# A new order for the 1551 steps of a clustered attention and gated MLP

## The chip, the cores and the metric

One core of a Trainium2 chip runs the whole kernel as one launch. The metric is device time in microseconds: the median of three runs of the kernel before is 299.8 us (299.25 to 300.07). In the text, PE is TensorE, DVE is VectorE, ACT is ScalarE, POOL is GpSimd and SP is SyncE, which here only issues transfers.

## The reference

There are 4 batches of 8 heads, with 768 tokens of 64 numbers each. Every query and key is assigned to the nearest of 16 centroids of its head, and a query attends only to the keys of its own cluster. The result, as 3072 tokens of 512 numbers, goes through an MLP with a SiLU between two matrices.

```python
q_assign = np.argmax(np.einsum('bhsd,hcd->bhsc', q_n, c_n), axis=-1)
k_assign = np.argmax(np.einsum('bhsd,hcd->bhsc', k_n, c_n), axis=-1)
mask = q_assign[:, :, :, None] == k_assign[:, :, None, :]
scores = scale * np.matmul(q, k.transpose(0, 1, 3, 2))
scores = np.where(mask, scores, -1000000000.0)
scores = scores - np.max(scores, axis=-1, keepdims=True)
attn = np.exp(scores)
attn = attn / (np.sum(attn, axis=-1, keepdims=True) + 1e-09)
attn_out = np.matmul(attn, v)
x = attn_out.transpose(0, 2, 1, 3).reshape(B * S, H * D)
h = x @ w_in                                  # (3072, 512) @ (512, 2048)
out = (h * (1.0 / (1.0 + np.exp(-h)))) @ w_out # (3072, 2048) @ (2048, 512)
```

## The kernel before, in words

The kernel has no loop over its work. It is cut into 1551 small steps, and a text called `plan` (line 722) lists them in the order in which they are issued. The function `step` (line 604) turns each word into instructions. Every engine takes its own instructions in the order of this list, so the plan fixes the order on PE, ACT, DVE, POOL and SP; between engines only semaphores order the work. A word is the step's name and number, then an engine where there is a choice (A for ACT, D for DVE, P for POOL), then one digit for each PSUM bank that the step opens. `qk50` is the score matmul 50, `hi1.A` is done by ACT, `pv4.3` uses bank 3.

A job is the q and k of one head, 128 partitions with 12 rows of 64 numbers each. Jobs k0 to k7 and x0, x1 hold batch 0, h8 to h31 the other 24 heads. A job passes through these steps:

- `r`, `xr` load it in f32, by SP (lines 92 and 94). The eight first jobs are loaded ahead of the plan. The buffers `raw` are few: h jobs share four of them by number modulo 4, and a load waits until `lo` of the job before it in that buffer is done.
- `hi` and `lo` split it into two f16 halves (lines 103 to 107 and 112).
- Jobs of batch 0 are transposed by PE (`tr`, line 135) and copied out of PSUM (`evk`, `evq`). Jobs from h8 on are transposed by the DMA (`ht`, line 121), issued on SP, into the buffer `ab`.
- `L` or `l` computes the 16 logits of every row on PE (line 159), `mx` and `ge` their maximum and a one-hot mark (lines 183 and 192). For h8 to h15, `cm` transposes the marks on PE, `ce` scales them out of PSUM and a transfer on SP puts them below the job in `ab` (line 235). For h16 to h31, `cs` (POOL, line 199), `cx` (a DMA transpose on SP, line 208) and `cv` (a transfer on POOL, line 212) do it. So one matmul yields score and mask.

Attention is cut into units `qk` (PE, line 325), two matmuls each, three units to a head and half of its queries. `ex` (ACT, line 330) takes the exponential; the scores have two PSUM buffers, so `qk` waits until the `ex` two units earlier is done. `vl` loads v (line 264, on SP, or on POOL with P), `v` casts it, `pv` (and its parts `pa`, `pb`, `pc`, `px`, `py`) multiplies (PE, line 342), `nm` divides, and `pt` with `pe`, or for later heads the DMA transpose `xd` on SP (line 381), brings the result into the form that the MLP reads.

The MLP has units `e` (PE, line 390; `a` is the first three quarters of one), `t` (tanh on ACT, line 402) and `g` (DVE, line 405). The second matrix is multiplied in the steps `b` and `bo` for the first two output tiles, and otherwise by a scheme with seven products for pairs of tiles: sums `S`, products `m` (PE, line 477), copies `z` and outputs `o`. `w0` to `w11` load the weights on POOL, each behind a tiny copy that waits for the last `ex` listed ahead of it (line 522). `wc` prepares sums of the second matrix. `j` steps are matmuls on zeros, which fill PE early on.

The transfers of SP go through one DMA queue (q1 in the profile) and those of POOL through another (q0). Both are served by the same 16 DMA engines of the core.

The lines that the steps of the prediction touch: 92 (loads), 121 (DMA transposes of jobs), 159 (logits), 235 (one-hot blocks), 264 (v), 325 (scores), 330 (exp), 526 and 529 (weights).

Of the kernel before, what the change touches and what calls it, by code (L numbers as in the profile page):

```python
# [29 lines left out]
def kernel(  # L30
# [573 lines left out]
    def step(op, n, eng, banks):  # L604
# [138 lines left out]
        t19 e25.2 g19 t25 cm12.1 qk53 ex53 e26.3 g25 v15.D qk54 t26 ex54 ce12.D vl16.P g26 e16.0 t16 e30.2 qk55 ge13
        g16 vl17.P l15.3 ls15 t30 ex55 lo16 r20 qk56 e28.0 t28 ex56 vl14 g30 e17.3 g28 L14.1 qk57 qk58 t17 g17 ex57
        cm13.2 mx14 e31.0 ce13.D ex58 qk59 t31 v9.D mx15 S3 m1.3 ge14 od2 hi17.A ex59 g31 ge15 wc13 pv8.2 cm14 lo17
        r19 ce14.A ht17 qk60 nm8 ex60 S1 qk61 ex61 m7 qk62 ex62 cm15.0 ce15.A wc7 S13 pv9.1 z0 qk63 ex63 S2 nm9 wc14
        v16.D wc9 wc15 wc10 qk64 m11.2 ex64 qk65 m2.0 qk66 ex65 m17 ex66 hi18.P qk67 qk68 lo18 z10 ex67 ht16 vl21.P
        wc11 wc3 S11 v17 S4 m6 pv10.1 ex68 z1 hi20.D qk69 ex69 qk70 ex70 m5 o0 qk71 ex71 l17.0 S12 m16 z2 nm10 z11
        ls17 qk72 vl19.P ht18 vl18.P hi19.A xd8 qk73 l16.0 od1 o3 ex72 r22 r21 ex73 m4 mx17 m15 z12 ls16 mx16 lo19
        qk74 qk75 lo20 v14 xd9 xd10 ge16 o13 pv11.1 nm11 ex74 ex75 ht19 qk76 ex76 m3 pt11.0 m14 S14 o2 r23 qk77 ge17  # L750
        cs16 o1 qk78 ex77 m12.3 qk79 o12 v18.A m13 ex78 qk80 ex79 o11 o10 pv12.3 hi22.D hi21.D lo21 v21 l18.2 ls18
        ex80 qk81 pe11.A ex81 cs17 e35.1 t35 g35 qk82 nm12 e33.0 ex82 qk83 ex83 e32.2 lo22 qk84 ex84 mx18 e34.3 t34
        qk85 g34 t33 g33 pv13.1 ex85 qk86 ex86 ge18 cs18 l19.3 cx16 nm13 e36.0 ht20 vl20 ls19 t32 g32 vl22 t36 g36
        qk87 ex87 cx17 ht22 hi23.D e37.1 qk88 t37 g37 mx19 xd12 ex88 cx18 e40.3 ht21 t40 lo23 cv16 g40 cv17 e39.0 qk89
        ex89 t39 e41.2 ht23 l20.1 qk90 ex90 ls20 mx20 g39 qk91 ge20 t41 ex91 g41 pv14.3 vl24.P e38.1 t38 g38 qk92 ex92
        qk93 nm14 e43.2 t43 ge19 g43 ex93 e42.0 l22.1 ls22 xd13 cs19 qk94 ex94 xd14 cx19 e44.3 mx22 t42 g42 cs20 qk95
        ex95 e46.1 l21.2 ls21 t46 g46 qk96 qk97 S23 pv15.0 ex96 cx20 qk98 r25 e47.1 mx21 ge21 e45.2 t44 cv18 nm15 g44
        ex97 qk99 ex98 t47 xd15 v22 t45 qk100 cs21 g47 g45 m21.0 ex99 ex100 v19.D ge22 l23.1 qk101 ls23 m22.2 z20
        qk102 ex101 ex102 qk103 ex103 m27.1 qk104 pv16.3 ex104 cv19 qk105 qk106 ex105 S21 S22 mx23 o20 v20 ex106 m26
        z21 S24 ge23 e48.2 t48 cx21 qk107 ex107 r24 cs22 cx22 cv20 qk108 nm16 m25 z22 o23 vl23.P pv17.3 cs23 hi24.D  # L760
        xd16 qk109 cx23 v23.D cv21 ex108 qk110 m23 cv22 ex109 g48 nm17 o21 m24 o22 ex110 qk111 lo24 ht24 e49.2 ex111
        qk112 e50.1 cv23 t49 vl25.P ex112 g49 qk113 xd17 e51.3 v24 t50 ex113 qk114 g50 e52.2 t51 pv18.0 ex114 g51 t52
# [67 lines left out]
```

## Time and profile before

| what | value |
|---|---|
| time, median of three runs | 299.8 us |
| span of the profiled execution | 297.9 us |
| instructions | 8577 |
| PE, matmuls | 3433, mean clock 1.000 |
| DMA bytes | 44.13 MB, 75208 packets |
| DMA queue q1 (SP) | 35.75 MB, 50.3% of 16 engines over the span |
| DMA queue q0 (POOL) | 7.54 MB, 13.5% |

The time of a run is a little more than the span, which goes from the first to the last instruction of one profiled execution; only that execution has a trace. A row of a group or a timeline gives the start in us, the duration in us (for several instructions in a row, from the first start to the last end), the engine, the line of the kernel, the operation, what is written and read, and the count. Matmuls overlap: the duration of one is longer than the distance to the next. A bracket at the end of a row says how long the engine was idle and what released it. In the chain of work that ended last, rows have the start, the length and the step. In the stretches, each engine's busy time stands with its number of instructions, and the DMA share is the mean busy share of the 16 DMA engines. In rows of DMA queues stand the packets, the MB and the share of 16 engines in that stretch. In rows of issues stand the number of transfers, the size of one and the median time from issue to landing.

### The profile page before, as it was taken

To read this page: it belongs to the slowest core of one execution; us is meant where nothing else is said; L and a number is where in the kernel's file an instruction comes from. 1 tells how busy PE (TensorE), PEld (TensorE's weight loads), DVE (VectorE), ACT (ScalarE), POOL (GpSimd) and SP (SyncE) were. 2 spreads that over 40 slices of the span, in tenths; PEclk is the share of its full clock that TensorE was granted. 3 is DMA by queue.
4 is the path that set the end of the run, shared out by engine and by line. 5 is a ranking of instruction groups with operands and counts; after the bars stand their busy time and mean duration, and the time that the engine had idled before them with its cause. 6 is when DMAs were issued, how large, how long until landed. Compare 5 with 4: busy or idle time off the path is not lost.

```text
span 297.9 us, 8577 instructions
## 1 busy us (share of the span) xinstructions
PE 288.7 (97%) x3433; PEld 212.6 (71%) x3433; DVE 223.8 (75%) x489; ACT 233.2 (78%) x406; POOL 68.7 (23%) x124
## 2 busy tenths in 40 slices
PE   7899999999979999999999999999999999999995
PEld 3767766666658887777866887767867886777684
DVE  5898849689979986989467897788656733666663
ACT  5998999965979878999789876898669768964731
POOL 2655804000227001334444024220420000000000
PEclk9999999999999999999999999999999999999999
DMA  6999999999997899795399535867221102211103
GB/s 214 286 256 247 179 201 176 193 247 216 171 300 178 171 176 257 176 151 131 102 202 213 164 66 114 256 165 113 51 89 35 26 2 74 82 29 35 39 19 125
DMA packets 75208, 44.13 MB, mean 148 GB/s; under 512 B 54288, under 2 KB 70960, under 8 KB 75168
## 3 DMA queue, kind: packets, MB, share of 16 engines
q1 hardware_dynamic: 70272, 35.75, 50.3%
q0 software_dynamic: 4608, 7.54, 13.5%
q8 instruction: 27, 0.44, 0.6%
q10 hardware_dynamic: 288, 0.30, 0.3%
q14 instruction: 13, 0.11, 0.1%
HBM read 27.30 MB, written 6.29 MB: 113 GB/s over the span
## 4 chain that ended last, share of the span: by engine, by line
PE 87%; DMA 5%; ACT 3%; DVE 3%; issue 1%; SPq 0%; ACTq 0%
PE ph L390 25%; PE pS L325 20%; PE xb L477 18%; PE pO L342 12%; PE psN L159 4%; PE yb L477 3%; PE po L417 2%; DMA ab<-cd 2%; DMA ab<-hl 1%; DMA raw<-in_q_dram 1%; DVE hl L112 1%; PE wb L477 1%; ACT P L330 1%; ACT hl L103 1%; PE pTq L135 1%
## 5 line engine op out<-in xcount | busy, mean ns | idle before, releaser
L330 ACT ACTIVATE P<-pS 128x768 f16<-128x768 f32 x192 | 151.0, 815 | 18.8 <-PE pS L325 17.4
L390 PE MATMUL ph<-xt,win_s 128*128 128x384 f16 x512 | 96.1, 326 | 0.0
L405 DVE SCALAR_TENSOR_TENSOR gt<-tn,ph 128x384 f16<-128x384 f32 x128 | 68.2, 549 | 31.9 <-ACT tn L402 31.0
L325 PE MATMUL pS<-ab 128*128 128x384 f16 x384 | 86.7, 326 | 2.2 <-DMA ab<-cd 1.6
L402 ACT ACTIVATE tn<-ph 128x384 f32<-128x384 f32 x128 | 61.6, 499 | 13.9 <-PE ph L390 10.5
L390 PEld LDWEIGHTS <-win_s 128*128 128x128 f16 x512 | 49.4, 98 | 31.0 <-issue 0.3
L325 PEld LDWEIGHTS <-ab 128*128 128x128 f16 x384 | 34.2, 98 | 18.3 <-DMA ab<-cd 2.2
L342 PEld LDWEIGHTS <-P 128*128 128x128 f16 x1152 | 39.8, 97 | 3.8 <-DVE cd L234 0.4
L342 PE MATMUL pO<-vt,P 128*128 128x65 f16 x1152 | 41.2, 193 | 0.0
L477 PEld LDWEIGHTS <-gt 128*128 128x128 f16 x352 | 34.1, 98 | 6.5
L112 DVE SCALAR_TENSOR_TENSOR hl<-raw,hl 128x768 f16<-128x768 f32 (+3 forms) x35 | 32.0, 916 | 0.8 <-ACT hl L103 0.5
L105 POOL TENSOR_SCALAR hl<-raw 128x768 f16<-128x768 f32 (+1 forms) x9 | 19.5, 2167 | 47.2 <-DVE gt L405 30.7
L477 PEld LDWEIGHTS <-s 128*128 128x128 f16 x264 | 25.5, 98 | 4.7
L199 POOL TENSOR_SCALAR od<-od 128x96 f16<-128x96 f16 x16 | 8.4, 526 | 63.3 <-DVE od L192 63.2
L499 ACT ACTIVATE ot<-xb 128x256 f32<-128x256 f32 x33 | 12.7, 385 | 12.9 <-PE xb L477 12.6
L477 PE MATMUL xb<-wout_s,gt 128*128 128x256 f16 x176 | 22.6, 273 | 0.0
L159 PEld LDWEIGHTS <-ab 128*128 128x128 f16 x544 | 18.9, 97 | 4.1 <-DMA ab<-hl 0.5
L477 PE MATMUL xb<-wc,s 128*128 128x256 f16 x160 | 20.7, 272 | 0.0
L159 PE MATMUL psN<-stk,ab 128*128 128x16 f16 (+1 forms) x544 | 20.1, 184 | 0.1
L354 DVE TENSOR_TENSOR xn<-pO,zr 128x384 f16<-128x384 f32 x32 | 17.8, 557 | 1.1
L490 DVE TENSOR_TENSOR s<-gt 128x1024 f16<-128x1024 f16 x22 | 15.5, 712 | 1.3 <-PE xb L477 1.0
L212 POOL DMA_DIRECT2D ab<-cdt x16 | 9.0, 564 | 19.8 <-PE pS L325 5.2
(93 smaller groups left out, 258.2 us busy)
## 6 DMA issues: line engine op xcount, KB each, us to landing
raw<-in_k_dram SPq DMA_DIRECT2D x31, 192.0 KB, 3.9
raw<-in_q_dram SPq DMA_DIRECT2D x24, 192.0 KB, 3.5
out_dram<-ot SPq DMA_DIRECT2D x18, 256.0 KB, 2.9
vn<-in_v_dram SPq DMA_DIRECT2D x19, 192.0 KB, 4.7
vn<-in_v_dram POOLq DMA_DIRECT2D x13, 192.0 KB, 3.4
win_s<-in_moe_w_in_dram POOLq DMA_DIRECT2D x8, 256.0 KB, 6.8
wout_s<-in_moe_w_out_dram POOLq DMA_DIRECT2D x4, 512.0 KB, 9.2
out_dram<-ot SPq DMA_DIRECT2D x12, 128.0 KB, 1.8
```

What stands on the lines that cost most here:

```text
L105: nc.gpsimd.tensor_scalar(out=o, in0=i, scalar1=QS, scalar2=None, op0=ALU.mult)
L112: nc.vector.scalar_tensor_tensor(out=hl[:, s, 1, :], in0=raws[job.name][:, s, :], scalar=QS, in1=hl[:, s, 0, :], op0=ALU.mult, op1=ALU.sub ...
L159: nc.tensor.matmul(L[:, n % 2, :, n // 2], ab[:, i, :], stk[:, job.groups[i // 3][0], x : x + w], start=(x == 0), stop=(x + w == 2 * HC),)
L325: nc.tensor.matmul(pS[:, e, 0:HALF], abs_[kj.name][:, kn, :], rhs, start=True, stop=True)
L330: nc.scalar.activation(out=P, in_=pst.pop(u)[:, :, 0:HALF], func=AF.Exp, bias=0.0, scale=ESC)
L342: nc.tensor.matmul(o[:, (2 * t + h) * VW : (2 * t + h + 1) * VW], Ps[i + h, c, j // 2][:, j % 2, ts(t, 128)], vtb[(i + h) % 13][:, j, 0:VW ...
L354: nc.vector.tensor_tensor(out=xn, in0=ov[:, :, 0:D], in1=zr.unsqueeze(2).to_broadcast([128, 2 * NM, D]), op=ALU.mult)
L390: nc.tensor.matmul(ph[:, 0:HALF], win_s[:, r, ts(fb, 128)], xts[b, c][:, r, :], start=(r == 0), stop=(r == NR - 1))
L402: nc.scalar.activation(out=tn, in_=phs[b, c, fb][:, 0:HALF], func=AF.Tanh, bias=0.0, scale=0.5)
L405: nc.vector.scalar_tensor_tensor(out=gt[:, fb, NM * c : NM * c + NM, :].rearrange("p t n -> p (t n)"), in0=tns.pop((b, c, fb)), scalar=1.0 ...
L477: nc.tensor.matmul(o, self.lhs(l, f), self.rhs(r, f), start=(f == 0 and opens), stop=(f == HB - 1), skip_group_check=True)
L490: nc.vector.tensor_tensor(out=o, in0=a, in1=b_, op=op)
```

## The change

The plan is replaced by another list of the same 1551 steps. Each step keeps its engine; the order and the PSUM banks differ. Two rules that depended on the order are made free of it: the three buffers of one-hot marks go to jobs in a fixed turn, and the five buffers of v go to the next load in the order in which they come free.

```diff
+    turn = """
+        k0 k1 k2 k3 k4 k5 k6 k7 x0 x1 h8 h10 h9 h11 h12 h13 h14 h15
+        h16 h17 h18 h20 h19 h21 h22 h23 h24 h26 h25 h27 h28 h29 h30 h31
+    """.split()
...
     def ge_n(job):
         m = (job.n + 1) // 2
-        nn[job.name] = len(nn)
+        nn[job.name] = turn.index(job.name)
...
-    vts, vns = {}, {}
+    vts, vns, vn_slot = {}, {}, {}
+    vn_free = list(range(5))
 
     def load_v(i, eng=nc.sync):
-        vn = mp.tile([128, NJ, D], f32, name="vn", bufs=5)
+        vn_slot[i] = vn_free.pop(0)
+        vn = mp.tile([128, NJ, D], f32, name="vn", tag=f"vn{vn_slot[i]}", bufs=1)
...
         vts[i] = vt
+        vn_free.append(vn_slot[i])
```

The first lines of the old plan, up to the third `ht`, and of the new one, up to the fourth:

```diff
-        j2.1 hi1.A lo1 vl3 hi2.D vl5 vl0 tr0.32 j2.0 evq0.A r8 vl1 evk0.A c5.12 stk lo2 vl4 kad tr1.03 L0.2 hi4.P w0
-        j2.1 mx0 ge0 evq1.A hi3.A lo3 evk1.A ct0.32 ctk0 tr2.10 ctq0 hi5.A evk2.A L1.3 lo4 xr0 evq2.A tr3.21 evq3.A
-        qk0 ex0 mx1 L2.0 ge1 ct1.13 ctq1 evk3.D qk1 ex1 L3.2 mx2 ge2 cm2 ce2.A ctk1 lo5 xr1 tr4.13 evk4.D evq4.A mx3
-        qk2 qk3 hi7.P v0 ge3 L4.0 mx4 ge4 tr5.31 ex2 qk4 v3.A ex3 hi6.P lo6 r10 vl7 cm3 evq5.D evk5.D ce3.A cm4 ce4.A
-        qk5 tr6.23 evk6.D ex4 L5.1 v5 evq6.D j1.2 qk6 vl2 L6.2 vl6 mx5 r9 r11 w1 lo7 tr7.03 ex5 ge5 qk7 xh0.A ex6 mx6
-        evk7.A ex7 qk8 cm5 ex8 xl0 ge6 cm6 ce5.D xq0.0 ce6.D evq7.D xp0.1 xu0.D qk9 xw0.D v1 vl12 ex9 v4 v7 pa0.3 qk10
-        w3 L7.1 w7 qk11 ex10 ex11 xL0.0 xM0 mx7 ge7 cm7 pb0 qk12 xm0 xg0 xh1.D ce7.A v2 xc0 pc0 xe0.D ex12 qk13 pa1.0
-        qk14 pc1 nm0 pt0.3 w2 ex13 qk15 xl1 w5 v6.D pb1 hi8.D nm1 ex14 qk16 ex15 qk17 ex16 ex17 hi10.P w10 xq1.1 xp1.2
-        xu1.D qk18 qk19 pa2.0 pb2 w6 w4 od0 v12.D xw1.D ex18 qk20 pt1.2 hi9.D pe1.D pc2 nm2 ex19 qk21 xL1.2 ex20 w8
-        xM1 ex21 qk22 qk23 pt2.0 ex22 ex23 xm1 px3.1 qk24 pe0.D lo8 xg1 xc1 py3 qk25 ex24 qk26 pe2.D a1.0 xe1.A nm3
-        pt3.1 pe3.D a0.2 ex25 ex26 qk27 ex27 e1 e4.1 e0 t4 g4 vl10 qk28 t0 g0 qk29 ex28 e6.3 t6 g6 ex29 vl11.P e3.1 t3
-        w9 t1 e5.2 qk30 ex30 w11 g3 lo9 r13 vl8 qk31 t5 pv4.3 qk32 ex31 nm4 e8.1 g1 g5 qk33 ht8 lo10 hi11.P e14.0 ex32
-        ex33 t14 g14 qk34 t8 ex34 qk35 e11.2 e13.3 ht10 g8 wc4 wc5 t11 g11 r12 ex35 t13 g13 qk36 ex36 e10.1 e15.0 qk37
-        pt4.2 qk38 e2.3 t10 ex37 ex38 lo11 pe4.D ht9 r14 pv5.2 g10 t15 nm5 qk39 qk40 t2 ex39 ex40 e7.1 e12.2 t12 ht11
...
+        vl1 hi1.A lo1 j2.0 j2.2 vl0 tr0.03 evq0.A evk0.A c5.12 kad stk tr1.30 hi3.A hi2.D lo2 hi4.P L0.1 mx0 ge0
+        evq1.A evk1.A tr2.20 evk2.A vl3 evq2.A ct0.13 ctq0 lo3 ctk0 lo4 L1.2 vl4 tr3.30 hi5.A xr0 qk1 r9 mx1 evq3.A
+        evk3.D ex1 L2.1 qk2 w0 vl2 ge1 hi6.P mx2 lo5 hi7.P L3.0 ct1.23 ex2 ge2 cm2 ctq1 qk0 mx3 ge3 cm3 j1.2 ctk1
+        ce2.A ce3.A w1 tr5.12 ex0 tr4.30 v3.A lo6 qk5 qk4 evq5.D evk5.D vl7 v1 evk4.D evq4.A xr1 tr6.21 ex5 L4.0 ex4
+        lo7 evk6.D v0 mx4 ge4 qk3 ex3 L5.3 mx5 cm4 ce4.A evq6.D L6.2 v4 ge5 cm5 ce5.D vl6 qk7 vl5 tr7.01 qk8 r8 pa0.3
+        w3 mx6 xh0.A ex7 evk7.A ge6 pc0 w7 w2 cm6 ex8 xl0 qk10 ex10 evq7.D L7.0 ce6.D qk11 mx7 xp0.1 ge7 ex11 v2 xu0.D
+        qk6 cm7 xq0.2 xh1.D ce7.A w5 pb0 qk9 xL0.1 w10 w6 xw0.D nm0 xM0 xm0 ex6 w4 ex9 qk15 ex15 w8 r10 pa1.0 qk16 pb1
+        w9 xg0 xc0 qk14 v5 ex16 xl1 ex14 pc1 xe0.D vl11.P hi9.D nm1 qk17 ex17 j2.1 r11 qk12 ex12 hi8.D v6.D xp1.2 qk13
+        ex13 xq1.3 pt0.1 xu1.D xw1.D qk20 ex20 xL1.2 qk18 ex18 pt1.3 lo9 pe1.D xM1 qk22 ex22 pa2.0 qk19 pb2 ex19 qk21
+        ex21 pc2 vl8 pe0.D qk23 ex23 px3.1 xm1 r13 xg1 nm2 lo8 qk24 ex24 pt2.0 pe2.D v7 py3 qk27 hi10.P ex27 nm3 ht9
+        hi11.P a0.3 xc1 xe1.A qk26 vl15 ex26 pt3.1 qk25 ex25 lo10 pe3.D e4.2 t4 g4 e0 t0 g0 e6.0 w11 t6 g6 v8.D qk28
+        ex28 ht8 a1.1 e1 lo11 qk29 e8.3 ht10 ex29 t8 vl13 qk32 ex32 e11.2 qk34 ex34 g8 t11 g11 e5.0 t5 hi13.D t1 g1
+        qk31 ex31 pv4.3 nm4 ht11 e15.2 t15 g5 qk38 ex38 qk42 ex42 g15 r12 e14.1 l9.3 t14 ls9 vl10 qk35 lo13 ex35 e13.0
+        t13 e3.3 t3 qk30 L8.2 ex30 g14 g13 qk33 ex33 e9.1 g3 e7.3 t9 mx8 ge8 cm8 mx9 t7 g9 g7 qk37 vl9 ex37 ge9 ce8.A
+        r14 qk36 e2.0 t2 g2 pv5.1 nm5 ex36 L11.2 hi12.A mx11 qk40 e10.3 v13.A qk43 ex40 b0.0 ge11 cm11 ex43 wc8 r15
...
```

Further down, the places that the prediction names, in the old list and in the new one:

```diff
-        hi12.A lo12 vl13 ht12 wc12 b4.3 ce10.A ex46 pt6.2 b5 cm9.0 ex47 hi14.A ce9.A pe6.A lo14 r16 pv7.1 nm7 b6 ht14
-        pt5.0 pe5.D qk48 hi15.D lo15 ht15 v10.D pt7.1 pe7.A r17 ex48 b7 bo1 e24.0 e18.1 t24 g24 t18 L11.2 wc8 mx11 g18
-        ge11 e22.3 t22 hi16.P e21.0 t21 g22 v11.D v8.D g21 qk49 qk50 cm11 ce11.D ex49 ex50 l12.3 vl9 ls12 e29.1 r18
...
+        lo12 wc9 t10 r17 v15.D ht12 vl18.P vl12 pt4.1 v10.D pe4.D qk39 ex39 b1 g10 qk44 pt5.1 ex44 qk46 ex46 L10.3
+        wc12 pe5.D ht13 qk41 ex41 e12.1 t12 mx10 ce11.D qk47 ex47 pv6.2 b2 hi14.A wc13 hi15.D ge10 cm10 qk45 ce10.A
...
+        ge12 l13.3 bo0 wc5 v11.D ht15 pt7.1 pe7.A ls13 b6 lo14 hi17.A qk57 ex57 b7 cm9.3 ce9.A lo17 ht17 cm12.1 bo1
...
```

More of the change, by code (lines that the diff above doesn't have):

```diff
@@ L743 @@
[L743 to L762, printed above, removed]
@@ new lines @@
+        ex92 g40 qk95 ex95 nm14 ge19 cs19 l21.1 ls21 cv18 e47.2 qk94 cx20 mx21 t47 vl22 e44.3 t44 ex94 g47 e45.0
+        hi24.D t45 g44 ge21 xd12 cx19 xd14 cs21 g45 e37.1 t37 xd13 cv19 vl20 qk96 e38.3 g37 ex96 cx21 t38 hi25.P g38
+        e42.2 t42 lo24 qk97 qk101 ex97 e43.0 r26 pv15.3 t43 ex101 v19.D qk99 ex99 S23 nm15 e46.1 t46 g42 qk100 mx22
+        ex100 g43 m21.3 qk104 ex104 l23.0 g46 qk98 ls23 m22.2 ht24 S21 S22 qk106 xd15 S24 cv21 ex98 qk102 ge22 ex106
+        z20 pv16.0 cv20 o20 ex102 lo25 qk107 ex107 cs22 cx22 mx23 m26 z21 qk111 ex111 nm16 ge23 r29 v22 e51.1 t51
@@ new lines @@
+        qk112 m25 m27.2 g51 z22 o23 cs23 ex112 cx23 qk105 ex105 m23 qk120 v20 ex120 cv22 o21 e53.0 hi27.D lo27 qk103
+        ex103 t53 g53 m24 o22 qk109 vl23.P hi26.P e49.1 ex109 t49 e52.3 g49 t52 g52 pv17.0 ht25 qk110 r28 ex110 nm17
+        l24.3 cv23 ls24 mx24 lo26 xd16 qk116 ex116 e55.2 t55 qk115 ex115 g55 e50.3 t50 g50 r30 xd17 qk117 ex117 e48.1
+        t48 g48 e62.2 qk113 ex113 qk108 e54.0 e56.1 e63.3 v23.D ex108 t54 t56 qk129 t63 g54 ex129 g56 ht27 vl25.P
+        qk131 ex131 ge24 g63 pv18.0 hi29.D e58.1 r31 t58 nm18 m41.3 ht26 qk118 qk119 g58 t62 ex118 vl29.P g62 ex119
@@ L795 @@
+        e118.3 t118 g115 t112 g112 g118 m83 e114.1 o81 t114 e127.0 t127 g114 g127 e113.2 t113 e120.3 g113 t120 g120
+        e119.1 e124.0 e121.2 e126.3 t119 g119 t124 g124 S93 t121 g121 e122.1 t126 g126 e125.0 t122 e123.2 t123 g122
+        t125 m91.3 m97 g123 g125 S91 S92 m101.2 m102.1 z90 m96 S103 m107.0 z100 S101 o100 z91 m95 z92 S94 S102 m106
+        m93 z101 m105 S104 z102 o91 o93 o103 m92.1 o90 m103 o101 m104 o102 m94 o92
     """.split()
```

75 lines of the change are left out of this document (40 added, 35 removed).

## The prediction

> **What bounds the kernel now.** I read the page first, then the chain that ended last, then the engines' shares in stretches of 10 us, then the DMA queues by stretch, and last the timelines of PE and SP around each place where PE waited.
>
> ```profile
> span 297.9 us, 8577 instructions
> PE 288.7 (97%) x3433; PEld 212.6 (71%) x3433; DVE 223.8 (75%) x489; ACT 233.2 (78%) x406; POOL 68.7 (23%) x124
> ```
>
> The sum is made against this span; the three runs have a median of 299.8 us, so 1.9 us lie around it, which I keep. PE is the bound and works in order, so what can change is how late it runs against its own work. The next rows, from the chain and from PE's timeline, price that work: the distance from one start to the next.
>
> ```profile
> 69.09 0.18 PE px L363 x3
> 90.24 1.10 PE pO L342 x36
> 277.00 5.20 PE ph L390 x32
> 293.55 0.89 PE xb L477 x8
> ```
>
> ```profile
> 58.16 1.03 PE L417 MATMUL po<-wout_s,gt 128*128 128x512 f16 x4
> 59.02 0.49 PE L325 MATMUL pS<-ab 128*128 128x384 f16 x2
> 59.35 0.76 PE L159 MATMUL psN<-stk,ab 128*128 128x16 f16 x24
> 59.95 1.02 PE L417 MATMUL po<-wout_s,gt 128*128 128x512 f16 x4
> ```
>
> A matmul of ph or pS costs 0.163 us, of pO 0.030, of po 0.215, of xb, yb or wb 0.109, a logit 0.025, a transpose 0.056; the whole plan comes to 280.1 us. I call a step's place the PE work listed ahead of it, and its lag the time at which it ran less its place. L8, the first logits of the second batch, has 149 transposes and the like, 208 logits, 90 pS, 216 pO, 64 ph, 8 po and 7 filling matmuls ahead: place 48.3. It ran at 59.35, a lag of 11.1. The last matmul ends at 294.4, a lag of 14.3, and 3.5 us of output follow: 280.1 + 14.3 + 3.5 = 297.9. Only the lag is to be won or lost. Where it grew:
>
> ```profile
> 64.16 0.51 PE L159 MATMUL psN<-stk,ab 128*128 128x32 f16 x12
> 74.83 0.52 PE L159 MATMUL psN<-stk,ab 128*128 128x32 f16 x12
> 87.46 0.82 PE L325 MATMUL pS<-ab 128*128 128x384 f16 x4 [1.57 <-DMA ab<-cd]
> ```
>
> l9 (place 53.0) ran with a lag of 11.1, l12 (63.3) with 11.6, qk57 (74.1) with 13.3. So the lag is made before 59 us and at one wait at 85.7; from 87.46 to the end it grows by 1.0. What feeds PE in that time is the DMA:
>
> ```profile
> core 0: us, PE busy (x) PEld busy (x) DVE busy (x) ACT busy (x) POOL busy (x), PEclk, DMA share, GB/s
> 0.00:10.00 10.00, 7.70 (x63) 3.87 (x63) 6.61 (x31) 6.15 (x12) 3.49 (x13) 1.00 0.74 229
> 10.00:20.00 10.00, 9.33 (x177) 7.37 (x176) 8.89 (x24) 9.73 (x18) 6.28 (x10) 1.00 0.96 289
> 20.00:30.00 10.00, 9.21 (x178) 7.07 (x177) 9.16 (x22) 8.62 (x12) 5.57 (x13) 1.00 1.00 233
> 30.00:40.00 10.00, 9.76 (x162) 7.20 (x161) 7.82 (x18) 9.38 (x13) 6.32 (x11) 1.00 1.02 174
> 40.00:50.00 10.00, 9.96 (x91) 6.33 (x90) 7.29 (x14) 9.72 (x19) 4.09 (x5) 1.00 1.00 197
> 50.00:60.00 10.00, 10.00 (x113) 6.51 (x111) 7.46 (x17) 9.42 (x17) 0.00 (x0) 1.00 1.18 192
> ```
>
> Its share is about 1.0 from 10 to 60 us: the 16 engines have no time to spare. PE hardly shows it, because the old list asks PE for each thing about when the DMA can have brought it.
>
> **The change part by part.** Both lists hold the same 1551 steps, each on the same engine with the same buffers' sizes. No work is added or removed; order, PSUM banks and slots differ.
>
> *Scores more evenly spaced.* Until the first MLP matmuls, exp on ACT paces PE. ACT's waits from 22 to 37.5 us in the old kernel:
>
> ```profile
> ACT P L330 <- PE pS L325: 1.1, 4, 0.6
> ```
>
> There the PE work from one qk to the next jumps between 0.3 and 1.4 us (qk16, qk17, qk18 at places 20.4, 20.7, 21.7); in the new list it is 0.6 to 1.1 from qk11 on. I credit 1.0 us; bounds 0 and 1.1.
>
> *The wait at 85.7 us.* It is an SP queue. DVE had written this one-hot block (h11) by 75.9; SP issued its transfer only at 82.05, behind two DMA transposes, a load and an output:
>
> ```profile
> 75.41 0.47 DVE L234 TENSOR_SCALAR cd<-psN,kadd 96x256 f16<-96x256 f32 x1
> ```
>
> ```profile
> 75.25 5.13 SPq L121 DMA_TRANSPOSE ab<-hl  x2
> 82.05 0.60 SPq L235 DMA_DIRECT2D ab<-cd  x1
> ```
>
> The new list has ht12 and ht13 ahead of ce11 on SP, but both stand well before it, and 8.9 us of PE work between ce11 and its first score (10.9 before). I credit 1.6 us, with bounds of 0 and 1.7.
>
> *Jobs of the second batch pulled forward: the cost.* ht9, ht8, ht10 and ht11 stood at places 41.6, 35.9, 38.5 and 44.6; they now stand at 27.4, 30.6, 32.2 and 35.5, and PE meets l9 at 37.5 (53.0 before), L8 at 39.8 (48.3), L11 at 44.5 (60.6). Place 44.5 is 148 transposes and the like (8.2), 244 logits (6.2), 80 pS (13.0), 216 pO (6.5), 56 ph (9.1) and 7 filling matmuls (1.5). Will the DMA have served them by then? Prices from the DMA queues by stretch: 0 to 30 us (loads on q1), 30 to 50 us (weights on q0), 56 to 59 us (transposes alone).
>
> ```profile
> q1 hardware_dynamic: 6017, 6.26, 65.8%
> ```
>
> ```profile
> q0 software_dynamic: 2297, 2.95, 87.9%
> ```
>
> ```profile
> DMA packets 2620, 0.69 MB, mean 231 GB/s; under 512 B 2600, under 2 KB 2619, under 8 KB 2619
> ...
> q1 hardware_dynamic: 2613, 0.67, 128.2%
> ```
>
> A load costs 0.658 x 30 / 6.26 = 3.15 us of all 16 engines per MB, a weight 0.879 x 20 / 2.95 = 5.96 us per MB, a transpose of 1536 packets 1.282 x 3 / 2600 x 1536 = 2.3 us. Sizes:
>
> ```profile
> raw<-in_k_dram SPq DMA_DIRECT2D x31, 192.0 KB, 3.9
> vn<-in_v_dram SPq DMA_DIRECT2D x19, 192.0 KB, 4.7
> win_s<-in_moe_w_in_dram POOLq DMA_DIRECT2D x8, 256.0 KB, 6.8
> wout_s<-in_moe_w_out_dram POOLq DMA_DIRECT2D x4, 512.0 KB, 9.2
> ```
>
> A head's q and k (two rows of 192 KB) cost 1.24, a v 0.62, all twelve weights 25.0. Old list, up to and with ht9, the third transpose: the first 8 jobs 7.4, x0 and x1 2.5, six r 7.4, twelve v 7.4, eight small one-hot blocks 1.2, weights 25.0, three transposes 6.9: 57.8 us. It landed here:
>
> ```profile
> L121 SPq DMA_TRANSPOSE ab<-hl x1: 2146/2146/2146, 58.8 to 58.8; - x1
> ...
> DMA to landing us min/median/max: 4.6/4.6/4.6
> ```
>
> So 57.8 us of listed work were done at 63.4: 5.6 us for the start, for holes and for the landing. New list, up to and with ht11: 7.4 + 2.5 + five r 6.2 + twelve v 7.4 + 1.2 + 25.0 + four transposes 9.2 = 58.9. With the same 5.6 that is 64.5, and L11 then has a lag of 20.0. Two things can make it earlier: w10, w8 and w9 stand at places 17.0 to 18.7 (21.0, 24.5 and 32.2 before), which can fill holes of the DMA, and w11 (3.1 us), listed at 30.3 behind hi10 and hi11 on POOL, can end behind ht11. The other weights will not make room. With both queues at work, q0 gets the larger part (48 to 54 us):
>
> ```profile
> q0 software_dynamic: 696, 0.70, 79.6%
> q1 hardware_dynamic: 461, 0.58, 31.9%
> ```
>
> The bounds are a lag of 15.5 (holes filled and w11 behind) and 20.0. I take 17.5, nearer to the middle, since the one row of this kind (63.4) has neither help. The wait comes in three or four pieces, at l9, L8 and L11, and at DVE's v8, lo11 and hi13, which stand in order behind the loads vl8, r11 and r13; gates queue behind those. The two gains above lie ahead of these waits or depend on the same DMA, and are swallowed. After L11 the list asks the DMA for less than it can serve.
>
> *Slots.* v's slot now comes from the earliest cast. Any waiting there is small already, and I put it at 0:
>
> ```profile
> SPq L264 <- DMA vn<-in_v_dram: 1.3, 1, 1.3
> ```
>
> The one-hot slots by a fixed turn and the other banks I put at 0 too; the cover is the 3 us or more of PE work between a slot's last reader and its next writer (cm8 at 42.0, ge11 at 47.3 in the new list). Without it, each would cost a fraction of a microsecond.
>
> *Sum.* Lag 17.5 after L11 in place of 13.3 after qk57, then the same 1.0: 280.1 + 18.5 + 3.5 = 302.1, and with 1.9 around it 304.0 us.
>
> **The rivals.** *The DMA keeps up (faster).* If the transposes land before PE asks, the gains stand: 297.9 - 1.0 - 1.6 = 295.3, or 297.2 us. It decides at l9: ht9 would have to land by about 47.6 (place 37.5 and a lag of 10.1). For it: nothing requires weights to be first. Against it: 79.6% to 31.9%, and the ledger.
>
> *It cancels (same).* From 47 to 60 us the transposes of the old kernel took:
>
> ```profile
> DMA to landing us min/median/max: 4.6/10.0/11.1
> ```
>
> If ht11 takes no more than 11.1, issued by SP at its place with the old lag (35.5 + 11.1 = 46.6), L11 runs at 57.7, a lag of 13.2, and 280.1 + 14.2 + 3.5 + 1.9 = 299.7.
>
> *PE cools down (slower still).* PE starts at half rate:
>
> ```profile
> 1.18 3.59 PE L538 MATMUL junk<-zz 128*128 128x512 f16 x8 [1.18 <-DVE zz L547]
> ```
>
> That is 0.45 us for a matmul of 512 columns against 0.215 for po. Should a long wait bring this back, it costs about half of 3.6 us once, 1.8: 305.8 us. The wait of 1.57 us above did not: the matmuls behind it have full rate. The Trainium skill, "TensorE: Matmul & The Clock Gate", Part 1, says that an idle window of about 3.4 us halves the clock until PE has been busy as long; by that rule a single wait over 3.4 us would do it, which no row of this trace can show.
>
> *Nothing of this is reached*, because order on POOL holds weights back: that falls under the first two.
>
> **How the numbers follow.** Forecast without cooling 0.48, with it 0.17, cancelling 0.10, DMA keeps up 0.25. A measurement of this kernel tells about 0.3%, 0.9 us. Faster 0.25, same 0.10, slower 0.65. The range goes from 297.2, the middle of the fast case, to 307.0, the upper bound of the lag (280.1 + 21.0 + 3.5 + 1.9 = 306.5) with some cooling. The slower case alone runs from 302 to 307.
>
> **What would show it.** Right: PE waits at psN for ab<-hl (L159) between 45 and 66 us, of 5 to 8 us in all; L11's 24 logits start at about 62; DVE waits for raw or vn near 40 to 48 us; a transpose takes over 11 us to land. Wrong: no wait of PE for ab<-hl, and L11 at 55; then the DMA served q1 ahead of the weights. The even spacing is right if ACT waits under 0.3 us for pS from 22 to 37 us.

## The result and the profile after

The new order takes 314.86 us (median of four runs, 314.01 to 322.95), the old one 299.52 us (299.09 to 300.07). The ratio is 1.0509, with a 95% interval of 1.0477 to 1.0541: slower by 15 us. (The run of 322.95 us is over 1.5% above the fastest of its kernel, so the median counts it and the ratio does not; the profiled execution of e3 below, of 316.45 us, is of the same kind.) The profiled execution of after took 315.52 us, with a span of 313.4 us. The head of its page:

```profile
span 313.4 us, 8562 instructions
PE 292.8 (93%) x3433; PEld 214.6 (68%) x3433; DVE 225.4 (72%) x489; ACT 234.7 (75%) x406; POOL 70.1 (22%) x124
```

PE has the same 3433 matmuls and 15.5 us more in which to run them. The stretches of 10 us say where (columns: stretch, its length, busy time of each engine, granted clock of PE, share of the DMA engines, GB/s):

```profile
core 0: us, PE busy (x) PEld busy (x) DVE busy (x) ACT busy (x) POOL busy (x), PEclk, DMA share, GB/s
30.00:40.00 10.00, 7.59 (x111) 5.81 (x110) 4.89 (x12) 6.30 (x10) 5.26 (x8) 0.83 1.13 243
40.00:50.00 10.00, 9.76 (x115) 6.64 (x112) 7.43 (x14) 9.55 (x17) 3.12 (x3) 1.00 1.25 204
50.00:60.00 10.00, 4.23 (x33) 2.36 (x30) 2.61 (x6) 3.36 (x6) 0.00 (x0) 0.78 1.24 197
60.00:70.00 10.00, 10.00 (x127) 6.62 (x125) 7.75 (x18) 8.16 (x15) 0.30 (x1) 0.88 0.56 143
```

Two stretches lose most of it, 30 to 40 and 50 to 60 us, and in both the clock is below 1.00. PE's timeline there, with the logits of heads 9, 8 and 11 behind (a bracket is the idle time before the row, and what ended it):

```profile
31.50 0.33 PE L371 MATMUL px<-ident,xn 128*128 128x128 f16 x3
34.24 0.50 PE L333 MATMUL pS<-ab 128*128 128x384 f16 x2 [2.41 <-DMA ab<-cd]
...
35.90 0.80 PE L333 MATMUL pS<-ab 128*128 128x384 f16 x2
36.49 0.87 PE L350 MATMUL pO<-vt,P 128*128 128x65 f16 x12
...
38.47 0.55 PE L333 MATMUL pS<-ab 128*128 128x384 f16 x2
...
50.08 0.81 PE L398 MATMUL ph<-xt,win_s 128*128 128x384 f16 x4
56.66 1.46 PE L333 MATMUL pS<-ab 128*128 128x384 f16 x4 [5.77 <-DMA ab<-cd]
57.92 1.49 PE L398 MATMUL ph<-xt,win_s 128*128 128x384 f16 x4
59.20 0.85 PE L159 MATMUL psN<-stk,ab 128*128 128x32 f16 x12
...
62.77 0.49 PE L333 MATMUL pS<-ab 128*128 128x384 f16 x2
63.10 0.75 PE L159 MATMUL psN<-stk,ab 128*128 128x16 f16 x24
...
67.83 0.76 PE L159 MATMUL psN<-stk,ab 128*128 128x16 f16 x24
```

Both waits are for one-hot rows of batch 0 (`ab<-cd`): at 34.24 for head 6, at 56.66 for the job x1. Behind each the matmuls run at half rate for a while (the granted clock is 0.50 from 36 to 38 and from 56 to 62 us): from 56.66 to 62.77 there are 18 matmuls of pS and ph and 12 logits, 3.2 us by the prices of the prediction, in 6.1 us, so 2.9 us are lost; from 35.90 to 38.47 it is 1.2 us. What x1's row waited for stands in SP's timeline, and in the landings of the first transpose and of the row:

```profile
36.52 8.07 SPq L121 DMA_TRANSPOSE ab<-hl  x1
44.70 0.70 SPq L240 DMA_DIRECT2D ab<-cd  x1
...
46.13 11.57 SPq L121 DMA_TRANSPOSE ab<-hl  x2
...
58.43 1.42 SPq L121 DMA_TRANSPOSE ab<-hl  x1
```

```profile
L121 SPq DMA_TRANSPOSE ab<-hl x1: 8075/8075/8075, 36.5 to 36.5; - x1
...
DMA to landing us min/median/max: 19.9/19.9/19.9
L240 SPq DMA_DIRECT2D ab<-cd x1: 702/702/702, 44.7 to 44.7; - x1
...
DMA to landing us min/median/max: 11.9/11.9/11.9
```

The transpose of head 9 (ht9) is listed just ahead of x1's row. It holds SP for 8.07 us and lands at 36.5 + 19.9 = 56.4; the row behind it is issued at 44.70 and lands at 56.6. In the old list no transpose of the second batch stood ahead of that row. Three smaller waits follow. The first and the last are for transfers; the second, of 0.54 us, is for DVE:

```profile
133.41 0.52 PE L159 MATMUL psN<-stk,ab 128*128 128x32 f16 x12 [1.50 <-DMA ab<-hl]
156.53 0.50 PE L333 MATMUL pS<-ab 128*128 128x384 f16 x2 [0.99 <-DMA ab<-cdt]
```

The account of PE's time: waits 2.4 + 5.8, half rate 1.2 + 2.9, later waits 1.5 + 0.5 + 1.0, and 0.8 more between the last matmul and the end, less the 1.6 us wait at 85.7 that is gone: 14.5 of the 15.5 us. The rest is in pieces under 1.3 us.

### The profile page after: what moved, and what is told of

The parts are those of the page before. It is cut to its first block, busy times and chain, and to the rows that moved or that the text cites. A ratio compares the mean times of both kernels' runs of the same rounds, so it can differ in the third digit from the quotient of the medians.

```text
span 313.4 us, 8562 instructions
## 1 busy us (share of the span) xinstructions
PE 292.8 (93%) x3433; PEld 214.6 (68%) x3433; DVE 225.4 (72%) x489; ACT 234.7 (75%) x406; POOL 70.1 (22%) x124
## 4 chain that ended last, share of the span: by engine, by line
PE 75%; DMA 13%; SPq 5%; DVE 3%; issue 2%; ACT 1%; POOL 1%; POOLq 0%; DVEq 0%; ACTq 0%
PE ph L398 22%; PE xb L485 17%; PE pS L333 16%; PE pO L350 10%; DMA ab<-cd 7%; PE psN L159 3%; PE yb L485 3%; PE po L425 2%; DMA ab<-hl 2%; DMA ab<-cdt 1%; DMA raw<-in_k_dram 1%; SPq L389 1%; SPq L213 1%; SPq L271 1%; PE wb L485 1%
## 5 line engine op out<-in xcount | busy, mean ns | idle before, releaser
L398 PE MATMUL ph<-xt,win_s 128*128 128x384 f16 x512 | 99.6, 330 | 0.3 <-DVE xt L382 0.2
L333 PE MATMUL pS<-ab 128*128 128x384 f16 x384 | 90.6, 331 | 9.2 <-DMA ab<-cd 8.2
L350 PEld LDWEIGHTS <-P 128*128 128x128 f16 x1152 | 40.5, 98 | 4.3 <-issue 0.7
L350 PE MATMUL pO<-vt,P 128*128 128x65 f16 x1152 | 42.0, 194 | 0.0
L507 ACT ACTIVATE ot<-xb 128x256 f32<-128x256 f32 x33 | 12.6, 385 | 15.7 <-PE xb L485 15.5
L107 DVE TENSOR_SCALAR hl<-raw 128x768 f16<-128x768 f32 (+1 forms) x16 | 10.8, 684 | 9.1 <-DMA ab<-hl 6.6
```

Of the source, the lines that this page charges most:

```text
L333: nc.tensor.matmul(pS[:, e, 0:HALF], abs_[kj.name][:, kn, :], rhs, start=True, stop=True)
L350: nc.tensor.matmul(o[:, (2 * t + h) * VW : (2 * t + h + 1) * VW], Ps[i + h, c, j // 2][:, j % 2, ts(t, 128)], vtb[(i + h) % 13][:, j, 0:VW ...
L398: nc.tensor.matmul(ph[:, 0:HALF], win_s[:, r, ts(fb, 128)], xts[b, c][:, r, :], start=(r == 0), stop=(r == NR - 1))
L507: nc.scalar.activation(out=o, in_=self.xb[:, 0:DH], func=AF.Copy, bias=0.0, scale=0.5)
```

## The experiments

Each run has a short name, e1 to e18. In the diffs a line holds steps of the list; a time without "before" beside it is a median, and each ratio is to the kernel before, run on the same chip at the same time. The theory: more transfers are listed ahead of the first readers than the DMA queues carry, so PE waits at whichever reader comes first. The main rival: two or three unlucky places in the order, on SP or on VectorE.

**The code without the order (e1).** The old list in the new code, so that only v's queue and the slots differ.

> The list of steps of before in the code of after: only the buffers of v from a queue and the fixed turn of the one-hot slots are new. Theory (all of the time is in the order of the list): 299.5 us, within 0.3% of before. Rival (the queue hands out a buffer of v that is still waited for, and a load behind it on SP or GpSimd is late): over 300.5 us, with more idle time of GpSimd at the lines that load v.

299.76 us, 1.0005 [0.9977, 1.0032]. All of the change's time is in the list.

**Is it the place of one transpose?** First ht9 behind x1's row (e3):

```diff
- nm3 ht9 hi11.P a0.3 xc1 xe1.A qk26
+ nm3 hi11.P a0.3 xc1 xe1.A ht9 qk26
```

> After with one step moved: the DMA transpose of head 9 goes behind the one-hot row of x1 on the SP queue, in place of ahead of it. Rival (one transfer stands in front of another on one queue, which is all that ails the order there): x1's row is issued at 42.5 us in place of 44.70 and without the transpose ahead of it, the 5.93 us wait at 50.57 us and the slow matmuls behind it (2.9 us) go, 306 to 309 us. Theory (what is listed by then is more than the queues carry): the wait moves to the logits of head 9 and 8, which need the transposes, and at least half of it stays: 310 to 315 us.

311.04 us, 1.0391 [1.0354, 1.0428], in the theory's range: by the ratios 3.5 of the 15 us came back. Its trace is left aside. In after something else waits at that place too, on DVE (waits from 36 to 62 us):

```profile
DVE hl L107 <- DMA ab<-hl: 6.6, 1, 6.6
```

The buffer that `hi13` writes is free when ht9 has landed, and gates of batch 0's MLP queue on DVE behind it. So e16 moves this step as well:

```diff
- e5.0 t5 hi13.D t1 g1 ... vl10 qk35 lo13
+ e5.0 t5 t1 g1 ... vl10 qk35 hi13.D lo13
```

> After with the transpose of head 9 behind x1's row on SP, and the high half of head 13 moved on VectorE from ahead of the gates of blocks 1 and 5 to its low half's place, 3 us of TensorE work later: so nothing of batch 0 stands behind the second batch's transposes any more at 49 us. Theory (more is listed than the queues carry, whichever step waits for it first): the wait moves on to the logits of head 9 or 8, at 51 to 56 us, 4 us or more, 308 to 312 us. Rival (the two places where batch 0 stands behind these transposes are the loss): no wait over 2 us between 45 and 65 us, 302 to 306 us.

316.07 us, 1.0553 [1.0492, 1.0615]: no gain over after. The wait has moved on, to the logits of head 9:

```profile
59.26 0.82 PE L159 MATMUL psN<-stk,ab 128*128 128x32 f16 x12 [6.36 <-DMA ab<-hl]
```

Freed of both places, PE runs into the transposes themselves. It is at l9 at the same time as in after (59.26 and 59.20 us). The time is above the theory's range, the place and the size of the wait are as it said; the rival with its 302 to 306 us is out. Why e16 takes 5 us more than e3, which has only the first of its two moves, stays open.

**Is it the amount?** The order of after, with fewer bytes of weights (e5):

```diff
-  wout_s[:, 4 * r : 4 * r + 4, :],
-  moe_w_out[512 * r : 512 * r + 512, :].rearrange("(c p) d -> p c d", p=128),
+  wout_s[:, 4 * r, :], moe_w_out[512 * r : 512 * r + 128, :]
+  nc.gpsimd.memset(wout_s[:, 4 * r + 1 : 4 * r + 4, :], 0.0)
```

> After with the four loads of w_out cut to a quarter (one block of rows in four; the other blocks are set to zero on GpSimd, and the last product is computed with these zeros, so three quarters of w_out are left out of the result). No step moves. The three loads that fall before 50 us shrink by 7.8 of the 10.4 us that they have in the ledger of transfers. Theory (too many bytes are listed ahead of the one-hot rows of batch 0): x1's row and the transposes of head 9 and 8 land several us earlier, the 5.93 us wait at 50.57 us falls below 2 us, with its slow matmuls gone: 303 to 308 us. Rival (the order on the SP queue by itself: a transpose issues for 8 us whatever else moves): the wait stays over 4 us, 312 to 316 us.

308.92 us, 1.0336 [1.0289, 1.0383]. The 5.8 us wait for x1's row is gone, with nothing moved. SP's timeline of this kernel:

```profile
38.00 2.98 SPq L121 DMA_TRANSPOSE ab<-hl  x1
44.10 0.58 SPq L240 DMA_DIRECT2D ab<-cd  x1
45.42 4.06 SPq L121 DMA_TRANSPOSE ab<-hl  x2
```

ht9 holds SP for 2.98 us in place of 8.07, the next two for 4.06 in place of 11.57. The long issue is thus an effect of what else is on its way. x1's row is issued hardly earlier than in after, at 44.10 us in place of 44.70; what went is its time to land:

```profile
DMA to landing us min/median/max: 2.2/2.2/2.2
```

In after it is 11.9 us, behind ht9, which lands 19.9 us after its issue there and 6.9 us here. The first wait, for head 6, stays (2.4 us): the w_in loads run there. By the ratios 5.2 of the 15 us came back. 308.92 is just above the theory's range of 303 to 308; a wait of 2.9 us for `ab<-hl` came up at a later logit. Then all twelve loads cut in the same way (e15):

> After with all twelve weight loads cut to a quarter (columns of w_in and blocks of rows of w_out; the rest is set to zero on GpSimd, so three quarters of both weights are left out of the result). No step moves. Theory (what costs in the first 70 us is bytes and transposes on the same engines; with w_out alone cut 6 us of the 16 came back): both waits of batch 0's rows fall below 1 us, no slow matmuls, and what is left over before is the later waits, 2 to 4 us, and the end: 299 to 304 us. Rival (the order of the steps on SP and VectorE costs by itself): a wait over 2 us stays before 70 us, 305 to 310 us.

309.3 us, 1.0344 [1.0309, 1.0378]. No wait for a DMA of over 1 us is left before 70 us, but a new one of my own making is there, 3.8 us for casts of v on GpSimd (`PE pO <- POOL vt`), where the zeroing runs. So this run shows that the waits follow the bytes, and not what is left without them. The time is in the rival's range, 10 us above the old list, and the wait of 3.8 us is less than half of that: it is not ruled out that the order costs something in other ways too.

**The weights' places.** After with the weights back at their old places (e2):

> After with the twelve weight loads put back at the places, in TensorE work listed ahead, that they have in the list of before (w10, w6, w4, w8 and w9 move by 4 to 14 us of TensorE work, w0 and w1 too); nothing else moves. Theory (the list asks for more transfers ahead of the one-hot rows of batch 0 than the queues carry, and the weights take the larger share): the row of head 6 lands in 5 us or less in place of 8.82, the 2.58 us wait at 31.61 us and the slow matmuls behind it go (2.6 + 1.5 us), and the 11.92 us of x1's row gets shorter by some us: 306 to 311 us. Rival (the transposes on the SP queue alone hold the rows up, the weights are beside the point): both waits stay, 313 to 316 us.

316.52 us, 1.0583 [1.0556, 1.0611]. The time is above both ranges. Head 6's wait went, as the theory said, but x1's row still takes 12.3 us to land, the MLP now waits for the second half of w_in, and L8 for its transpose:

```profile
47.10 1.46 PE L398 MATMUL ph<-xt,win_s 128*128 128x384 f16 x4 [5.07 <-DMA win_s<-in_moe_w_in_dram]
55.20 0.82 PE L333 MATMUL pS<-ab 128*128 128x384 f16 x4 [1.11 <-DMA ab<-cd]
62.89 0.82 PE L159 MATMUL psN<-stk,ab 128*128 128x16 f16 x24 [3.51 <-DMA ab<-hl]
```

The new list needs its weights early. Given them late, it waits for them instead. The converse, the old list with early weights (e10):

> The list of before with the twelve weight loads at the places that they have in after (w10, w6, w4, w8 and w9 4 to 13 us of TensorE work earlier). Nothing else moves. Theory (the weights are one part of what overfills the queues; the old list leaves 4 us between the landing of x1's row at 44.2 us and its first use): the rows of batch 0 land later, one wait of 1 to 3 us before 35 us, 300 to 304 us. Rival (the queues have room here as long as the second batch is not pulled forward): within 0.3% of before, 298.2 to 300 us.

308.49 us, 1.0319 [1.0289, 1.0348], more than either theory said, and for a third reason. GpSimd works in order, and each weight load stands behind a tiny copy that waits for an exponential:

```profile
13.47 0.18 POOL L522 COPY pace<-P 1x1 f16<-1x1 f16 x1 [3.28 <-ACT P L330]
...
26.58 0.18 POOL L522 COPY pace<-P 1x1 f16<-1x1 f16 x1 [6.34 <-ACT P L330]
```

Behind it queue casts of v and high halves, for which PE and VectorE then wait. This run says nothing on the DMA; it shows that weights cannot be moved on GpSimd by themselves.

**The second batch's places.** In e9 the old list, with the steps of heads 8 to 15 where after has them (and a few MLP blocks were moved behind a free bank):

```diff
- xc1 py3 qk25 ex24 qk26 pe2.D a1.0 xe1.A
+ xc1 py3 qk25 hi10.P ht9 hi11.P ex24 qk26 pe2.D a1.0 vl15 xe1.A
...
- e13.3 ht10 g8 wc4 wc5 t11 g11
+ l9.3 ls9 vl10 lo13 e13.3 g8 wc4 wc5 t11 g11
```

> The list of before, in which only the steps of the second batch's heads 8 to 15 (loads, halves, transposes, logits, one-hot rows, buffers of v) stand at the places, in TensorE work listed ahead, that they have in after; the transpose of head 9 is back ahead of x1's row and those of heads 8, 10 and 11 stand 5 to 9 us earlier. The weights and batch 0 stay as in before. Theory (pulling the second batch forward is what costs, since more is listed than the queues carry): a wait of 3 us or more between 36 and 62 us, for x1's row or for the logits of heads 9, 8 and 11, and with the slow matmuls behind it 306 to 313 us. Rival (the early weights and batch 0's own new order are needed for the loss as well): no wait over 1.5 us there, 299 to 302 us.

321.68 us, 1.0739 [1.0667, 1.081], above the theory's range: pulling the second batch forward by itself, with these few MLP blocks, costs 23 us, more than the whole change. PE waited 6.6 us for a gate behind `hi13` and 4.6 us for L8. The stretches from 48 us, here and in before:

```profile
48.00:54.00 6.00, 0.00 (x0) 0.00 (x0) 1.34 (x4) 0.71 (x1) 0.00 (x0) 0.92 1.38 111
54.00:60.00 6.00, 4.96 (x26) 2.66 (x26) 2.29 (x5) 2.77 (x5) 0.00 (x0) 0.52 1.26 122
```

```profile
48.00:54.00 6.00, 6.00 (x70) 4.11 (x69) 5.01 (x11) 6.00 (x12) 1.12 (x1) 1.00 1.12 214
54.00:60.00 6.00, 6.00 (x57) 3.59 (x55) 4.42 (x11) 5.42 (x10) 0.00 (x0) 1.00 1.23 183
```

The DMA engines are as full in both, but carry 111 to 122 GB/s in place of 183 to 214: in e9 the transposes beside late weights get through slowly. Next, how many transposes x1's row bears ahead of it in the old list: one (ht8, e12), two (ht8 and ht10, e13) and three (ht9 too, e14).

```diff
- pe2.D a1.0 xe1.A
+ pe2.D a1.0 ht8 xe1.A
+ pe2.D a1.0 ht8 lo10 ht10 xe1.A
+ pe2.D a1.0 ht8 lo10 ht10 lo9 ht9 xe1.A
```

> The list of before with one step moved: the DMA transpose of head 8 goes ahead of x1's one-hot row on the SP queue (7.6 us of TensorE work earlier). Rival (one transpose ahead of that row is all it takes, as its issue holds SP for 8 us in after): the row is issued at about 46 us in place of 38.5 and lands at 52 us or later, against a first use at 48.3 us: a wait of 3 to 8 us there, 303 to 310 us. Theory (the issue takes so long only where more transfers are ahead of it than here): the transpose holds SP for 2 to 4 us, the row lands by 48 us, no wait over 1 us, 298.5 to 300.5 us.

> The list of before with the DMA transposes of heads 8 and 10 (and the low half of head 10 on VectorE) moved ahead of x1's one-hot row on SP; with head 8 alone the row was issued at 41.97 us and the time fell by 0.3%. Theory (there is room for about one transpose beside the weights; each further one holds SP for 5 to 8 us): the row is issued at 47 to 50 us and lands at 53 to 57 us, a wait of 4 to 8 us at 48 to 49 us, 303 to 308 us. Rival (a transpose ahead of the row is harmless in the old order, only the new places of all the second batch's steps together cost): no wait over 1 us, 297 to 299.5 us.

> As the run with two transposes, and the transpose of head 9 (with its low half on VectorE) ahead of x1's one-hot row as well, three in all. Theory (each further transpose holds SP for 5 to 8 us while weights are on their way): the row is issued 5 to 10 us later than with two, a wait of 9 to 16 us, 308 to 316 us. Rival: no wait over 1 us, 297 to 299.5 us.

One: 297.95 us, 0.9973 [0.995, 0.9996]. Two: 302.83 us, 1.0115 [1.0062, 1.0168]. Three: 310.49 us, 1.0366 [1.0322, 1.0411]. SP's timelines of the three, in this order:

```profile
36.37 5.50 SPq L121 DMA_TRANSPOSE ab<-hl  x1
41.97 0.57 SPq L235 DMA_DIRECT2D ab<-cd  x1
```

```profile
37.05 9.63 SPq L121 DMA_TRANSPOSE ab<-hl  x2
46.78 0.59 SPq L235 DMA_DIRECT2D ab<-cd  x1
```

```profile
37.27 17.95 SPq L121 DMA_TRANSPOSE ab<-hl  x3
55.32 0.58 SPq L235 DMA_DIRECT2D ab<-cd  x1
```

The row is issued at 41.97, 46.78 and 55.32 us, and PE waits 0.4, 4.40 and 9.96 us for it. The first transpose is free, though it holds SP for 5.50 us and not for the 2 to 4 us that were expected: it uses up the room that the row had, and it leaves the crowded stretch behind it with one less. Each further one costs about what it holds SP: 4.1 and 8.3 us, against 4.2 and 7.5 us in the time by the ratios. This is the theory's picture, with the point from which it counts. The first of these kernels, e12, is 0.3% below the old list, with an interval that just leaves out 1; e18 below, which has the same move, does not show this gain again.

**The clock.** Matmuls on zeros in the two waits, 11 and 30 (e4):

```diff
+ j11.0 qk20
+ j30.1 qk38
```

> After with 11 matmuls on zeros ahead of the scores that wait at 31.61 us and 30 ahead of those that wait at 50.57 us (2.4 and 6.5 us of TensorE work that nothing reads), so that TensorE does not stand still in the two waits. Theory (each of the two waits slows TensorE's clock for some us, 1.5 and 2.9 us by the spacing of the score matmuls, .32 us in place of .163): the granted clock stays at 1.0 from 30 to 65 us and the time falls by 2.9 to 4.4 us, to 310.5 to 312 us. Rival (the slow matmuls cost nothing, since the next transfer is what the work waits for in any case): no change, 314 to 316 us.

322.17 us, 1.0768 [1.0697, 1.0839], above both ranges. The first fill kept the clock at 1.00 from 30 to 40 us (0.83 in after):

```profile
30.00:40.00 10.00, 9.01 (x127) 5.96 (x126) 5.15 (x13) 6.46 (x10) 4.74 (x8) 1.00 1.12 240
```

Yet it brought nothing, for the landing of ht9 set the time as before. The second fill's bank was read by a gate behind `hi13`, so it ran only when the wait was over, and its 6.5 us came on top. In e6 the fill has a bank that is free, ahead of block 15, and the first fill is left out:

```diff
- nm4 ht11 e15.2 t15
+ nm4 ht11 j24.2 e15.2 t15
```

> After with 24 matmuls on zeros (5.2 us of TensorE work that nothing reads) ahead of the last matmul of block 15, 0.65 us before the scores that wait at 50.57 us, on a bank whose last reader runs before that wait. The end of the wait is set by a transfer, so the fill takes its place. Theory (standing still halves TensorE's clock, and the slow matmuls behind the wait cost 2.9 us): granted clock 1.0 from 56 to 63 us, 311.5 to 312.5 us. Rival (the time behind the wait is set by the next transfers, the slow clock hides in it): 314 to 316 us, with a wait at the logits of head 9 or 8 in place of the slow matmuls.

PE's timeline of this kernel:

```profile
49.64 5.34 PE L546 MATMUL junk<-zz 128*128 128x512 f16 x24
55.04 0.81 PE L398 MATMUL ph<-xt,win_s 128*128 128x384 f16 x4
56.58 0.82 PE L333 MATMUL pS<-ab 128*128 128x384 f16 x4 [0.74 <-DMA ab<-cd]
57.57 0.81 PE L398 MATMUL ph<-xt,win_s 128*128 128x384 f16 x4 [0.16 <-DVE gt L413]
```

The row landed when it did in after, and the matmuls behind it ran at full rate (0.81 us for four of ph, 1.49 in after). The span of this execution is 310.2 us, 3.2 less. The median is 315.97 us, 1.0582 [1.0531, 1.0633], but the four runs lie too far apart to tell: 312.32, 314.65, 317.30 and 317.99 us, against 314.01 to 315.52 in after. That half rate follows the wait, and that the fill keeps it off, is shown; what it costs in the time stays open.

**The later part.** Old steps up to a point, then the new order: at 63.1 us of work (e8), then at 95.3 (e11).

> The first 425 steps of the list of before (63.1 us of TensorE work), and behind them the other 1,126 steps in the order of after, with the banks that they have there. Theory (all of the loss arises in the first 45 us of work, and the later waits at 131.59, 148.69 and 155.27 us, 3.5 us in all, come from the lateness that the transfers were left with): 298 to 300.5 us. Rival (these later waits belong to the order of the new list in its later part): 302 to 304 us, with waits of 0.7 to 1.7 us at the same three places in the work (108.8, 123.9 and 129.6 us listed ahead).

> The first 625 steps of the list of before (95.3 us of TensorE work), and behind them the other 926 steps in the order of after. Theory (the later waits of after, 1.67 us for the logits at 108.8 us of work and 0.71 and 1.15 us at 123.9 and 129.6, belong to the order of its later part, since every kernel so far that holds this part has two or three of them): the same waits, 2 to 4 us in all, 301 to 303.5 us. Rival (they come from the lateness of the first part): none of them, 298 to 300 us.

316.33 us, 1.0584 [1.0546, 1.0623], and 314.93 us, 1.0538 [1.0484, 1.0592]. Neither answers its question. Where the lists meet, the MLP blocks that the new list has between a one-hot row and its scores were done already, and PE waited 10.8 us for head 11's row; in the second, VectorE stood 9.0 us at a `hi` for a buffer (`DVE hl <- DMA ab<-hl`) and PE 6.9 us behind it. Behind the joins both still have waits of PE at two of the three places of after's later ones, 0.6 and 1.0 us in e8, and 0.4 and 1.4 us in e11. After with the first of these places relieved, ht22 behind ht20 (e17):

```diff
- cx16 ht22 qk88 ... ex89 ht20 qk81
+ cx16 qk88 ... ex89 ht20 ht22 qk81
```

> After with one step moved: the DMA transpose of head 22 goes behind that of head 20 on SP, in place of ahead of it (both issued as one pair at 126.00 us for 4.01 us). The logits of head 20 wait 1.67 us at 131.59 us for their transpose; in the list of after they stand 2.0 us of TensorE work behind it, in that of before 3.5 us. Theory (the later waits are the new list's own, too little work between a transpose and its logits): the wait falls by about 2 us to none, the time by 1.0 to 1.7 us beside after, ratio to before 1.045 to 1.049. Rival (the late transfers of this stretch only move to the next reader, head 22 or the one-hot rows): ratio 1.048 to 1.054, with a wait at the logits of head 22 or later.

315.4 us, 1.054 [1.0516, 1.0563]. The wait for head 20 is gone, and the next row waits for it:

```profile
155.24 0.50 PE L333 MATMUL pS<-ab 128*128 128x384 f16 x2 [2.64 <-DMA ab<-cdt]
```

The rival was right: here too it is no single place.

**The wait at 85.7 us.** The old list with ht15 behind head 11's row, alone (e7) and with ht8 ahead of x1's row (e18):

```diff
- hi15.D lo15 ht15 ... cm11 ce11.D
+ hi15.D lo15 ... cm11 ce11.D ht15
```

> Before with one step moved: the DMA transpose of head 15 goes behind the one-hot row of head 11 on the SP queue, in place of ahead of it. Theory (the 1.73 us wait at 85.71 us is this queue's order, and it is there in most executions): the row is issued some 2.5 us sooner, the wait goes and 1.0 to 1.7 us stay gone to the end: 297.4 to 298.2 us beside 299.1 of before. Rival (the wait is there in some executions alone, as the run of the list of before in the code of after, which had none at this place, suggests): within 0.3% of before, 298.5 to 299.5 us.

> The list of before with both single moves on SP that can be had for nothing: the transpose of head 8 ahead of x1's one-hot row (0.9973 of before alone), and the transpose of head 15 behind the one-hot row of head 11 (no gain alone). Theory (the first one moves a transpose out of the crowded stretch at 48 us, the second one adds nothing): 297.5 to 298.5 us, ratio 0.995 to 0.999. Rival (both waits count, the one at 85.71 us is there in some executions): ratio 0.990 to 0.994.

299.7 us, 1.0032 [1.0005, 1.0058], and 299.28 us, 0.9995 [0.9975, 1.0015]. No gain from this move. Nor does e18 show the 0.3% of e12, so that gain is not established.

## Why the prediction was right in direction and wrong in size

*The cause* of the loss before 63 us was right: the second batch pulled forward meets DMA engines without time to spare. e9 shows that this step costs by itself, e5 that the bytes beside it matter, e12 to e14 the price per transpose. That q0 gets the larger part held as well (DMA queues of after, 44 to 54 us):

```profile
q0 software_dynamic: 1156, 1.28, 86.8%
q1 hardware_dynamic: 1225, 0.33, 38.5%
```

*The step that failed* is in "Jobs of the second batch pulled forward": "The wait comes in three or four pieces, at l9, L8 and L11, and at DVE's v8, lo11 and hi13". The ledger gave 60.0 to 64.5 us for the landing of ht11, and it landed at 58.43 + 4.1 = 62.5. But a lag is the largest of landing less place over all readers, and I took it at L11. x1's row, a step of batch 0 that hardly moved itself, is behind ht9 on the same queue, and its first reader, qk38, is at place 36.2 (l9's 37.5 less four ph and four pS). It landed at 56.62: a lag of 20.4. With the 2.9 us of half rate behind it that is 23.3, and L11 ran at 67.83, a lag of 67.83 - 44.5 = 23.3, against 17.5 forecast. When ht11 landed, PE was no longer waiting for it. I had followed the moved steps' own readers, not the readers of what now stands behind them. e16 shows the predicted wait, at l9 and of 6.36 us, once these others are out of its way. The "5 to 8 us in all" at psN was thus the right amount at the wrong reader. Of the signs that the prediction named, the slow landing came (19.9 us for ht9); in after PE has no wait for `ab<-hl` between 45 and 66 us, and DVE's wait there is not for a load but for a buffer of `hl`.

*The price of a transpose*, 2.3 us from a stretch without weights, is too low beside them. From the row of q1 above, 0.385 x 10 / 1225 x 1536 is 4.8 us, with a few loads' packets in it. In e9, the kernel with the second batch's places alone, 48 to 60 us,

```profile
q1 hardware_dynamic: 2072, 0.70, 90.0%
q0 software_dynamic: 679, 0.67, 40.4%
```

it is 0.90 x 12 / 2072 x 1536 = 8.0 us. At 4.8 us, four transposes cost 10 us more than in the ledger. That ht11 nevertheless landed at 62.5 is only in part the work of the early weights, one of the two helps that the prediction named: in e2, with the weights late, ht11 lands at 66.3 us. What makes up for the rest isn't shown, so it was partly luck that the landing fell into the ledger's range.

*"Then the same 1.0" to the end* was the second miss of size. The last matmul ended at 309.1, a lag of 29.0, so 5.7 us were added: 3.0 in the three waits, the rest in small pieces. e17 shows that such a wait, relieved at one reader, comes up at the next. Whether it is the same shortage is not shown: the DMA share in after is 0.99 around the first of them (126 to 134 us), 0.50 around the second (142 to 150 us) and 0.84 around the last (150 to 158 us). With 0.8 us more at the end, 5.8 + 4.7 + 0.8 = 11.3 us is the difference between 302.1 and the span of 313.4.

*Cooling* was a rival at 1.8 us, once; it came twice, 1.2 and 2.9 us in the trace, the first behind a wait of only 2.41 us. The Trainium skill, "TensorE: Matmul & The Clock Gate", Part 1, gives an idle window of about 3.4 us; here the shorter wait was followed by a clock of 0.83 in its 10 us, and the 1.57 us wait in before was not.

*Evenly spaced scores*, credited with 1.0 us and then held to be swallowed: ACT waited 3.0 us for pS from 22 to 37 us, 2.5 of it the wait for head 6. No gain is seen; by itself it wasn't tried.

*The wait at 85.7 us*, credited with 1.6: it is gone in after, but it was no fixed cost of the old list. It is in two of seven traces that have this stretch of the old order (before and e11, not e1, e10, e12, e13 and e14), and the kernel that removes its cause gains nothing. I had read a stable cost from one execution.

*Slots and v's queue* at 0: e1 confirms it.
